# A two-branch attention kernel: where its units of maxima are done, who splits one weight, and which PSUM set serves the query tiles

## Chip, cores and metric

The kernel runs on one core of a Trainium2 chip. The metric is the device time of one execution in microseconds (us); the time before is the median of three runs. Engines: PE multiplies matrices, ACT (ScalarE) does activations and copies, DVE (VectorE) elementwise work and reductions, POOL (GpSimd) elementwise work on SBUF alone, SP (SyncE) issues the DMAs.

## What is computed

`x` has 2048 tokens of 448 numbers, everything in float32. Two attention branches with 16 heads of 28 are mixed by a gate:

```python
g = sigmoid((x * gate_w).sum(-1, keepdims=True))
# branch A: linear attention with learned features
phi_q = concat(softmax(q @ w_phi), softmax(-(q @ w_phi)))      # the same for k
kv = einsum("bhsf,bhsd->bhfd", phi_k, v);  z = phi_k.sum(s)
a = (phi_q @ kv / (phi_q @ z + 1e-6)) @ wo_A
# branch B: full softmax attention, q, k, v from another weight
b = softmax(q @ k.T * 28**-0.5) @ v @ wo_B
return g * a + (1 - g) * b
```

## The kernel before

Tokens are tiled by 128 (16 tiles) or 512 (4 blocks), heads in 4 groups of 4. Precise products are made of two halves: a weight or an input is split into a rounded copy (`high`, on ACT as a rule) and the rest (`low`, a subtraction on DVE as a rule), `split_weight` L140, and three products of the halves are added; a tile of 448 columns is so 11 matmuls (`x3`, `tok_major`).

The order of PE, DVE, ACT and POOL is written out by hand: each engine runs its instructions in the order in which the code emits them. Only SP's queue of DMAs is ordered by a planner. `lows`, `exps`, `subs`, `diffs` are lists of instructions that are emitted later, when `take_lows` and its like are called.

The stages, in order of time:

1. Projections of branch B's q and k (`proj_qk`, n = 4 to 19, L663 on). At n = 16 and 18, `split_part` (L611) splits the two halves of wvA.
2. One loop over i (L726), with t = i the key tiles of branch A (i = 0 to 15) and q = i - 16 the query tiles (from i = 16 on), y = q - 1. A key tile does pk (keys), pva (values and gate), features and their sums into `pkv`. In the first twelve key tiles every second also does one more `proj_qk`.
3. At q = 2, the turn: `kv_copy` takes `pkv`, the pool of PSUM tiles is closed and opened again (L748 to L750) with four banks for the tag "s" in place of three for "s" and one for "pv". The query tiles do pq, features (`features1`: maxima on DVE, subtractions on POOL and, up to q = 8, on DVE; an exponential on ACT; `features2`: sums on DVE, a product on POOL), transposes (`turn`, pft), numerators (`numer`, pn). The numerators are normalized in four steps over the following tiles (`normalize1` to `normalize4`: copies oUa on ACT, denominators dena to DRAM and, repeated, back as rsa, a multiplication oUa on DVE, casts oTa on ACT and subtractions oTa on POOL), and `out_a` (poa, L556) applies the output weight. From q = 18 on, `value_b` (pvb) makes branch B's values of tiles 0 to 7. wvB is split at q = 14 and 17 (L804); its subtractions are emitted one tile later.
4. Last values: `value_b` of tiles 8 to 15 (L909), and the stacks for the scores (memsets, loads).
5. Scores, exponentials and values of branch B over 256 steps (L1115 on); `bank` hands out PSUM banks in the order of the lists `free`, `used`, `held`.

Softmax in branch B needs a maximum for each query ahead of the scores. For the first 44 pieces that is done by `mx_unit` (L258), which is called from stages 1 to 4: four matmuls of 28 rows side by side, two into `pmb`, two into `pmd` (L284), a relu of pmd on ACT (L287), two sums with a running maximum on DVE (L289). pmb and pmd take two PSUM banks each of four, so a unit needs the banks of the unit before. The rest of the maxima is done beside the scores (`mx_visit`, L304). Which unit comes next is counted in `mxs["u"]`; the loads of later pieces (`pair_query`, `mx_query`, `mx_load`) hang on that count. Units 0 to 3 are called at n = 16 to 19, then two for a pair of key tiles (one ahead of the pair, one by `tick` L718 in the middle of its 44 passes), one each at q = 0 and 1, one each at q = 8 to 18, two each from q = 19 on until all are done at q = 24. What is left would be done among the last values (L907 on); there, `psn[1]` is 3, and pmd has a tag of its own.

Of the kernel before, what the change touches and what calls it, by code (L numbers as in the profile page):

```python
# [14 lines left out]
PSUM = bass.MemoryType.PSUM  # L15
# [24 lines left out]
def gated_mix_kernel(ctx, tc, xT, wqkB, wvB, wvA, wkAT, wqAT, phi, woA, woB,  # L40
# [17 lines left out]

    psn = [3, 2]

    def ps_s(nm):
        return ps.tile([P, 512], F32, tag="s", name=nm, bufs=psn[0])

    def ps_pv(nm):
        return ps.tile([P, 512], F32, tag="pv", name=nm, bufs=1)
# [74 lines left out]
    def split_weight(w, raw, bs, cs, low=nc.vector, high=nc.scalar.copy):  # L140

        high(w[:, 0, bs, cs], raw)
        lows.append(lambda: low.tensor_sub(w[:, 1, bs, cs], raw, f32(w[:, 0, bs, cs])))
# [464 lines left out]
    def part_loads(key, src, n, nm):  # L608
        loads(key, lambda: load_part(src, n, nm, 0), lambda: load_part(src, n, nm, 2))

    def split_part(w, key, n, i, low=nc.vector):  # L611
        split_weight(w, raws[key][i], slice(2 * i, 2 * i + 2), slice(0, n), low)

    def splits(n):

# [47 lines left out]
    for n in range(4, NP):  # L663
        take_acts()
        if n in (4, 5):
            x_loads(n - 2)
        if n == 8:
            nc.sync.dma_start(phi_s, phi)
            load_fold(wkAT, "k")
        if n == 10:  # L670
            part_loads("wB1", wqkB[:, :, 512:896], 384, "wB1")
        splits(n + 1)
        if n == 14:
            part_loads("wvA", wvA, 450, "wvA")
            nc.sync.dma_start(sel_s, sel)
            nc.sync.dma_start(mask_s, mask)
            for v in vap:
                nc.gpsimd.memset(v[:, :, 28:32], 0.0)
                nc.gpsimd.memset(v[:, :, 28:29], 1.0)
            feats = [bd.tile([P, H, 64], F32, name=f"feat{i}") for i in range(4)]  # L680
            for f in feats:
                nc.gpsimd.memset(f[:, :, 56:], 0.0)
        if 16 <= n < 20:
            mx_unit()
        proj_qk(n, ev)
        if n in (16, 18):
            split_part(wvA_s, "wvA", 450, (n - 16) // 2)
            take_lows()
        if 12 <= n < 16:
            fold(wkA_s, "k", n - 12)  # L690
        if n == 10:
            pair_query(0, 0)
            pair_load(0, 0)
        if n == 15:
            pair_load(0, 1)
            pair_query(0, 1)
        if n in (14, 19):
            take_subs()
# [27 lines left out]
    for i in range(2 * NT + 11):  # L726
        t, q = i, i - NT
        y = q - 1
        tb = y // 2
        take_acts()  # L730
        if t < NT and t % 2 == 0:
            mx_unit()
            passes = (55 if t < NT - 4 else 44) + (4 if t >= 4 else 0)
            pace["n"], pace["at"] = 4 if t >= 4 else 0, [passes // 2]
        if q in (0, 1):
            take_exps()

        if t % 2 == 0 and 0 <= t - 4 < NT:
            kv_add(t - 4)
            kv_add(t - 3)  # L740
        if q == 2:
            bk_s.close()
            ta_s = ExitStack()
            ta = ta_s.enter_context(tc.tile_pool(name="ta", bufs=1, reuse_waits="tile"))
            stg = ta_s.enter_context(tc.tile_pool(name="stg", bufs=2, reuse_waits="tile"))
            KV = ta.tile([P, 512], F32, name="KV")
            kvT = kv_copy()
            ps_s_.close()  # L748
            ps = ps_s_.enter_context(tc.tile_pool(name="psq", bufs=1, space=PSUM, reuse_waits="tile"))
            psn[0] = 4  # L750
            woA_s = weights(3, "woA_s")
            wvB_s = weights(2, "wvB_s")
            take_exps()
        if t < NT:
            pk = ps_s(f"pk{t}")
            tok_major(pk, t, wkA_s, D, tick)
            fk[t] = features1(pk, f"k{t}", nc.gpsimd)
            take_exps(1)
        if 0 <= q < NT:
            pq = ps_s(f"pq{q}")  # L760
            tok_major(pq, q, wqA_s, D)
        if q == 0:
            fk[NT - 1] = features2(fk[NT - 1], f"k{NT - 1}")
        if q in (1, 2):
            fq[q - 1] = features2(fq[q - 1], f"q{q - 1}")
        if 0 <= q < NT:
            fq[q] = features1(pq, f"q{q}", nc.vector if 0 < q < 9 else nc.gpsimd)
        if 0 <= t - 1 < NT - 1:
            fk[t - 1] = features2(fk[t - 1], f"k{t - 1}")
        if q in (0, 1) or q >= 8:  # L770
            mx_unit()
        if y >= 9 and y % 2 and tb - 4 < 8:
            oTs[tb - 4] = normalize4(ta, num.pop(tb - 4), f"a{tb - 4}", 2)
        if y >= 4 and y % 2 == 0 and tb - 2 < 8:
            numer(tb - 2)
        if q > 0:
            take_exps(int(q < NT))
        if q == 3:
            kv_out(kvT)
        if 2 <= q - 1 < NT:  # L780
            fq[q - 1] = features2(fq[q - 1], f"q{q - 1}")
        take_subs()
        if t == 1:
            pair_load(0, 3)
        if y >= 8 and y % 2 == 0 and tb - 4 < 8:
            num[tb - 4] = normalize3(*num[tb - 4], 2)
        if t < NT:
            value_a(t)
            if t % 2 and t < NT - 4:
                proj_qk(NP + t // 2, ev)  # L790
        if q in (0, 1):
            proj_qk(NP + 6 + q, ev)
        take_lows()
        if 2 <= i < 6:
            fold(wqA_s, "q", i - 2)
        if q == 1:
            ev_s.close()
        if q == 2:
            raws["woA"] = [load_woA(b) for b in (0, 2)]
        if q == 11:  # L800
            part_loads("wvB", wvB, D, "wvB")
        if q in (4, 6):
            split_part(woA_s, "woA", D, (q - 4) // 2)
        if q in (14, 17):  # L804
            split_part(wvB_s, "wvB", D, (q - 14) // 3)
        if q == 1:
            gates()
        if y < 9 or y % 2:
            if y >= 2 and y - 2 < NT:
                turn(y - 2)  # L810
        if 0 <= y - 10 < NT:
            out_a(y - 10)
            out_a2(y - 10)
        if y >= 9 and y % 2 == 0 and y - 2 < NT:
            turn(y - 2)
        if NT + 3 <= q < NT + 10:
            mx_unit()
        if q == NT + 2:
            bd_s.close()
            vb = [value_tile(0)]  # L820
        if 0 <= q - NT - 2 < 8:
            value_b(q - NT - 2)
        if y >= 5 and y % 2 and tb - 2 < 8:
            num[tb - 2] = normalize2(ta, *num[tb - 2], f"a{tb - 2}", 2, True)
# [78 lines left out]
    ps_s_.close()  # L903
    ps = ps_s_.enter_context(tc.tile_pool(name="psv", bufs=1, space=PSUM, reuse_waits="tile"))
    psn[:] = 2, 3
    rlp = fr_s.enter_context(tc.tile_pool(name="rlp", bufs=1, reuse_waits="tile"))
    mx_unit()  # L907
    rest = NF - mxs["u"]
# [17 lines left out]

    free, used, held = list(range(7)), [], []
    spare = []  # L930

    def bank(i, nm):
# [289 lines left out]
```

## Time and profile before

| what | us |
|---|---|
| median of 3 runs (1024.96 to 1025.58) | 1025.13 |
| the profiled execution | 1025.96 |
| its span, from the first to the last instruction | 1024.2 |
| PE busy / DVE / ACT / POOL | 1013.9 / 680.7 / 820.0 / 236.2 |

The times of a timeline count from the span's start; a timeline's row has start, length, engine, line, operation, out<-in, shape and count, and in brackets how long the engine stood idle before it and what ended that. A row of busy time by stages has the stretch, its length, the busy time (and count) of PE, PEld (weight loads), DVE, ACT and POOL, then the mean granted clock of PE, the DMA share and GB/s. Key tiles run from 64 to 171 us, query tiles from 171 on, the last values from 318 to 337, the scores from there to the end.

### The profile page before, as it was taken

Reading aid. Unit: us, or ns where it says so; the run is one execution under the profiler, and the core shown is the slowest. Engines: PE = TensorE matmul, PEld = TensorE weight load, DVE = VectorE, ACT = ScalarE, POOL = GpSimd, SP = SyncE. Lnnn points to the kernel's source line nnn. Section 1 sums busy time; section 2 is a strip of 40 time slices with the busy share of each in tenths; the row PEclk is TensorE's granted clock in tenths of the full one; section 3 lists DMA queues with packets and bytes.
Section 4 is the critical chain, followed back from the end, with each engine's and each line's share of the span. In section 5 each row is a group of like instructions: output and inputs, shape, how many; then the busy total and the mean of one; then the engine's idle time right before and its main releaser. Section 6 shows DMA issues by size and latency. Waiting matters only on the chain.

```text
span 1024.2 us, 18042 instructions
## 1 busy us (share of the span) xinstructions
PE 1013.9 (99%) x6472; PEld 557.3 (54%) x6472; DVE 680.7 (66%) x1340; ACT 820.0 (80%) x1534; POOL 236.2 (23%) x213
## 2 busy tenths in 40 slices
PE   9999999999999999999999999999999999999998
PEld 8878888868779433333333333333333333354555
DVE  6566567987753588788888787887878887710102
ACT  5445445677752999999999999999999999969672
POOL 1245546678435003111011110101201101011010
PEclk9999999989999999999999999999999999999999
DMA  8973110132345713233532133522313355414401
GB/s 297 310 238 93 52 52 1 61 73 81 94 129 132 146 26 77 69 68 72 123 79 72 42 74 74 128 58 55 89 42 77 87 129 140 121 58 125 132 32 54
DMA packets 64250, 98.89 MB, mean 97 GB/s; under 512 B 18176, under 2 KB 24944, under 8 KB 64160
## 3 DMA queue, kind: packets, MB, share of 16 engines
q1 hardware_dynamic: 64160, 97.74, 35.4%
q8 instruction: 51, 0.84, 0.4%
q14 instruction: 39, 0.32, 0.1%
HBM read 69.54 MB, written 27.78 MB: 95 GB/s over the span
## 4 chain that ended last, share of the span: by engine, by line
PE 89%; DVE 4%; DMA 4%; ACT 1%; SPq 1%; issue 1%; POOL 0%; DVEq 0%; ACTq 0%; POOLq 0%
PE st L871 29%; PE pv L998 25%; PE pm L321 9%; PE pk L126 4%; PE pva L126 4%; PE poa L108 4%; PE pob L108 3%; PE pq L108 2%; PE pqk L108 2%; DMA qkd<-ev 2%; PE pvb L126 2%; PE pvb L108 2%; PE pmb L284 1%; PE pft L524 1%; DVE rl L289 1%; DMA wvA_raw<-in_wvA_dram 1%
## 5 line engine op out<-in xcount | busy, mean ns | idle before, releaser
L889 ACT ACTIVATE p<-st 128x512 f32<-128x512 f32 x1020 | 525.7, 609 | 29.5 <-PE st L871 27.9
L332 DVE TENSOR_REDUCE part<-pm 128x1 f32<-128x512 f32 x477 | 304.8, 686 | 111.1 <-PE pm L321 104.7
L871 PE MATMUL st<-qst,kst 128*128 128x512 f32 x1024 | 315.5, 430 | 0.5 <-ACT vb L714 0.5
L998 PE MATMUL pv<-p,vb 128*32 128x512 f32 x2048 | 272.7, 605 | 0.0
L871 PEld LDWEIGHTS st<-qst,kst 128*128 128x128 f32 x1024 | 173.0, 187 | 137.5 <-issue 75.8
L321 PEld LDWEIGHTS pm<-kc,qc 28*128 28x128 f32 x848 | 40.5, 181 | 177.8 <-ACT p L889 169.4
L325 ACT ACTIVATE rl<-pm 128x512 f32<-128x512 f32 x212 | 126.9, 599 | 11.0 <-PE pm L321 0.3
L419 POOL TENSOR_TENSOR oUb<-oUb,rsb 128x512 f32<-128x512 f32 x15 | 19.3, 1289 | 467.4 <-DMA rsb<-rdb 229.9
L329 DVE CUSTOM_DVE_ANT_0 rl<-pm,rl 128x512 f32<-128x512 f32 x159 | 108.3, 681 | 0.0
L321 PE MATMUL pm<-kc,qc 28*128 28x512 f32 x848 | 107.1, 495 | 0.0
L998 PEld LDWEIGHTS pv<-p,vb 128*32 128x32 f32 x2048 | 40.3, 108 | 67.3 <-issue 63.1
L289 DVE CUSTOM_DVE_ANT_0 rl<-pmb,rl 128x512 f32<-128x512 f32 x88 | 57.1, 686 | 29.4 <-ACT rl L287 29.4
L1009 DVE SCALAR_TENSOR_TENSOR acc<-pob,gate,acc 128x448 f32<-128x448 f32 x12 | 8.2, 684 | 86.2 <-PE pob L108 86.2
L108 PE MATMUL pqk<-XH,wB 128*128 128x512 f32 x192 | 59.3, 397 | 0.0
L287 ACT ACTIVATE rl<-pmd 128x1024 f32<-128x1024 f32 x44 | 45.2, 1028 | 12.2 <-PE pmd L284 5.6
L588 ACT CAST ev<-pqk 128x512 fp32r<-128x512 f32 x28 | 16.1, 588 | 36.1 <-PE pqk L108 30.2
L108 PE MATMUL poa<-woA_s,oTa 128*128 128x448 f32 x192 | 43.2, 374 | 0.0
L108 PEld LDWEIGHTS pqk<-XH,wB 128*128 128x128 f32 x192 | 35.4, 188 | 8.5 <-issue 1.5
L108 PE MATMUL pq<-wqA_s,XH 128*128 128x448 f32 x128 | 38.1, 381 | 0.8 <-DVE ev L589 0.8
L195 POOL TENSOR_TENSOR kc<-kc,kd 28x512 fp32r<-28x512 f32 x12 | 15.4, 1281 | 101.9 <-PE pm L321 50.7
L108 PEld LDWEIGHTS poa<-woA_s,oTa 128*128 128x128 f32 x192 | 35.1, 188 | 6.0 <-issue 3.3
L589 DVE TENSOR_TENSOR ev<-pqk,ev 128x512 fp32r<-128x512 f32 x28 | 19.0, 690 | 28.4 <-ACT ev L588 28.3
(159 smaller groups left out, 1176.8 us busy)
## 6 DMA issues: line engine op xcount, KB each, us to landing
qkd<-ev SPq DMA_DIRECT2D x28, 512.0 KB
qst<-qkd SPq DMA_DIRECT2D x64, 224.0 KB
kst<-qkd SPq DMA_DIRECT2D x64, 224.0 KB
od<-oTb SPq DMA_DIRECT2D x48, 112.0 KB
rsa<-rda SPq DMA_DIRECT2D x8, 512.0 KB
rsb<-rdb SPq DMA_DIRECT2D x15, 256.0 KB
kc<-qkd SPq DMA_DIRECT2D x64, 56.0 KB
gad<-ga SPq DMA_DIRECT2D x16, 224.0 KB
```

The lines of the kernel that those rows point to most:

```text
L108: nc.tensor.matmul(dst, l, r, start=i == 0, stop=i == len(todo) - 1)
L126: nc.tensor.matmul(dst[:, :n], l, r, start=i == 0, stop=i == len(todo) - 1, skip_group_check=True)
L287: nc.scalar.activation(rl, pd, AF.Relu)
L289: nc.vector.tensor_tensor_reduce(rl[:, i, :], pb[:, i, :], rl[:, i, :], 1.0, LOWEST, ALU.add, ALU.max, part[:, col + i:col + i + 1])
L321: nc.tensor.matmul(pm[j], mxs[("qc", gq)][js, qt * P:(qt + 1) * P], mxs[("kc", g, kb)][js, :], start=True, stop=True, tile_position=(32 * ...
L325: nc.scalar.activation(rl, pm[kb], AF.Relu if kb < 3 else AF.Copy)
L329: nc.vector.tensor_tensor_reduce(r, pm[j], r, 1.0, LOWEST, ALU.add, ALU.max, part[:, col + j:col + j + 1])
L332: nc.vector.tensor_reduce(part[:, col + j:col + j + 1], pm[j], AX.X, ALU.max)
L419: (nc.gpsimd if n == 1 else nc.vector).tensor_mul(oU, oU, rs)
L871: nc.tensor.matmul(st, kst_of[(g, kt // 4)][:, j, (kt % 4) * P:(kt % 4 + 1) * P], qst_of[gq][:, j, :], start=True, stop=True)
L889: nc.scalar.activation(p, st, AF.Exp, scale=SCALE)
L998: nc.tensor.matmul(pv[32 * j:32 * j + 32, :], vb[kt // 8][:, kt % 8, 4 * g + j, :], pt[j], start=kt == 0, stop=kt == NT - 1, tile_position ...
```

## The change

- The units: pairs of key tiles 4, 6 and 8 have two units by `tick`, at a third and two thirds of their passes, in place of one in the middle; query tiles 8, 9 and 10 have none; from q = 19 on there is one a tile in place of two. So 41 units are done when the loop ends, and three are left to the last values.
- wvA is split by POOL, both halves.
- wvB is split at q = 13 and 15 in place of 14 and 17.
- At the turn the PSUM pool is kept: every fourth tile that asks for "s" gets the bank of "pv". This ends at the last values.
- `free`, the list from which the first banks of the scores are taken, begins in another order.

```diff
+    turn4 = []
+
     def ps_s(nm):
+        if turn4:
+            turn4.append(nm)
+            if len(turn4) % 4 == 0:
+                return ps_pv(nm)
         return ps.tile([P, 512], F32, tag="s", name=nm, bufs=psn[0])
...
-    def split_part(w, key, n, i, low=nc.vector):
-        split_weight(w, raws[key][i], slice(2 * i, 2 * i + 2), slice(0, n), low)
+    def split_part(w, key, n, i, low=nc.vector, high=nc.scalar.copy):
+        split_weight(w, raws[key][i], slice(2 * i, 2 * i + 2), slice(0, n), low, high)
...
         if n in (16, 18):
-            split_part(wvA_s, "wvA", 450, (n - 16) // 2)
+            split_part(wvA_s, "wvA", 450, (n - 16) // 2, nc.gpsimd, nc.gpsimd.tensor_copy)
             take_lows()
...
             mx_unit()
             passes = (55 if t < NT - 4 else 44) + (4 if t >= 4 else 0)
-            pace["n"], pace["at"] = 4 if t >= 4 else 0, [passes // 2]
+            pace["n"] = 4 if t >= 4 else 0
+            pace["at"] = [passes // 3, 2 * passes // 3] if t in (4, 6, 8) else [passes // 2]
...
-            ps_s_.close()
-            ps = ps_s_.enter_context(tc.tile_pool(name="psq", bufs=1, space=PSUM, reuse_waits="tile"))
-            psn[0] = 4
+            turn4.append("")
...
-        if q in (0, 1) or q >= 8:
+        if q in (0, 1) or q >= 11:
             mx_unit()
...
-        if q in (14, 17):
-            split_part(wvB_s, "wvB", D, (q - 14) // 3)
+        if q in (13, 15):
+            split_part(wvB_s, "wvB", D, (q - 13) // 2)
...
-        if NT + 3 <= q < NT + 10:
-            mx_unit()
...
     psn[:] = 2, 3
+    turn4.clear()
...
-    free, used, held = list(range(7)), [], []
+    free, used, held = [0, 2, 3, 4, 5, 1, 6], [], []
```

## The prediction, made before the run

> **What bounds the kernel now.** I read the page first (busy shares, chain), then busy time by stages, the waits of PE, and the timelines of the other engines where a wait stands. Times are us from the span's start.
>
> ```profile
> PE 1013.9 (99%) x6472; PEld 557.3 (54%) x6472; DVE 680.7 (66%) x1340; ACT 820.0 (80%) x1534; POOL 236.2 (23%) x213
> ...
> PE 89%; DVE 4%; DMA 4%; ACT 1%; SPq 1%; issue 1%; POOL 0%; DVEq 0%; ACTq 0%; POOLq 0%
> ```
>
> ```profile
> 64.00:171.00 107.00, 107.00 (x960) 90.07 (x958) 66.25 (x139) 52.30 (x89) 58.51 (x50) 1.00 0.23 69
> ...
> 211.00:229.00 18.00, 15.90 (x129) 11.61 (x128) 15.32 (x33) 11.91 (x20) 14.45 (x12) 0.81 0.38 97
> ...
> 337.40:1018.00 680.60, 680.48 (x4096) 284.52 (x4097) 462.31 (x928) 631.24 (x1235) 65.30 (x62) 1.00 0.33 82
> ```
>
> PE is busy nearly throughout and is nearly the whole chain. The second view (busy PE, PEld, DVE, ACT, POOL, then the granted clock) shows where it isn't: 211 to 229 has 2.1 us idle and a clock of 0.81. From 337.4 on (scores and values, two thirds of the time) the change touches nothing but the start. PE's work stays the same, so the forecast is a sum over PE's waits before 337.4: which go, which come.
>
> Nearly all are one wait. A unit of maxima is matmuls into pmb and pmd (0.43 of PE in all), a relu on ACT (1.03) and two sums on DVE (1.23). Unhindered, pmd starts beside pmb; hindered, it waits until DVE has left the unit before. A bracket in a row is PE's idle time; it leaves out the 0.5 in which pmb alone ran, so the wait is the bracket + 0.5.
>
> **Part by part.**
>
> *wvA split by POOL.* Units stand 3.2 apart here, and two are held up:
>
> ```profile
> 56.36 0.50 PE L284 MATMUL pmd<-kp,qp 28*128 28x512 f32 x2 [0.68 <-DVE part L289]
> ...
> 63.59 0.50 PE L284 MATMUL pmd<-kp,qp 28*128 28x512 f32 x2 [0.34 <-DVE part L289]
> ```
>
> ```profile
> 53.01 0.95 ACT L142 CAST wvA_s<-wvA_raw 128x900 fp32r<-128x900 f32 x1 [0.34 <-DMA wvA_raw<-in_wvA_dram]
> ```
>
> ```profile
> 58.41 2.66 POOL L220 TENSOR_TENSOR kp<-kp,kt 28x512 fp32r<-28x512 f32 x2 [10.87 <-DMA kt<-qkd]
> ```
>
> ```profile
> L428 POOL TENSOR_TENSOR oTb<-oUb,oTb 128x512 fp32r<-128x512 f32 x15 | 19.3, 1287 | 1.2
> ...
> L427 POOL CAST oTb<-oUb 128x512 fp32r<-128x512 f32 x15 | 9.2, 613 | 0.9
> ```
>
> The waits are 1.18 + 0.84 = 2.0. Without ACT's cast and DVE's subtraction between its steps, a unit is through in 3.0, and they go. POOL, idle for 10.9 before 58.41, takes the work: scaled by columns (900/512) a cast is about 1.0 and a subtraction 2.3, so two of each from 53.0 end at 59.5, and the subtractions of kp queued behind them at 62.1. The first key tile's unit needs those and would start at 61.6: a new wait of 0.5. Net **-1.5**; bounds -2.0 (no wait) and 0 (POOL a third slower).
>
> *Three more units on key tiles 4 to 9*: **+1.3** of PE (3 x 0.43). Their cover:
>
> ```profile
> 113.16 0.50 PE L284 MATMUL pmb<-kp,qp 28*128 28x512 f32 x2
> ...
> 120.23 0.50 PE L284 MATMUL pmb<-kp,qp 28*128 28x512 f32 x2
> ```
>
> ```profile
> 115.44 0.69 DVE L289 CUSTOM_DVE_ANT_0 rl<-pmb,rl 128x512 f32<-128x512 f32 x1
> ```
>
> A unit is through 3.0 after its start (113.16 to 116.1), and they stand 7.1 apart. With three a pair they stand 4.5 to 5.1 apart, and two of the three now come right behind a key tile's copy, exponentials, maxima and sums, which I add up to 3.8 and 4.3. That fits, by 0.2 at the tightest; I take no wait.
>
> *The turn and query tiles 8 to 10.* Rows of PE, DVE, ACT, POOL and of the DMAs:
>
> ```profile
> 183.91 0.68 PE L108 MATMUL pq<-wqA_s,XH 128*128 128x448 f32 x2 [0.83 <-DVE ev L589]
> ...
> 206.95 0.50 PE L284 MATMUL pmb<-kp,qp 28*128 28x512 f32 x2
> ...
> 210.64 0.50 PE L284 MATMUL pmb<-kp,qp 28*128 28x512 f32 x2
> 213.25 0.79 PE L284 MATMUL pmd<-kp,qp 28*128 28x512 f32 x2 [2.10 <-DVE part L289]
> ...
> 221.38 1.10 PE L524 MATMUL pft<-ident,feat 128*128 128x128 f32 x8
> ...
> 225.11 1.11 PE L538 MATMUL pn<-fT,KV 56*32 56x256 f32 x32
> 226.15 2.73 PE L108 MATMUL poa<-woA_s,oTa 128*128 128x448 f32 x12
> 228.71 1.04 PE L524 MATMUL pft<-ident,feat 128*128 128x128 f32 x8
> ```
>
> ```profile
> 211.89 0.68 DVE L289 CUSTOM_DVE_ANT_0 rl<-pmb,rl 128x512 f32<-128x512 f32 x1
> ...
> 213.12 1.07 DVE L458 TENSOR_REDUCE fsumq<-feat 128x32 f32<-128x896 f32 x1
> ...
> 217.92 1.09 DVE L458 TENSOR_REDUCE fsumq<-feat 128x32 f32<-128x896 f32 x1 [0.71 <-ACT feat L451]
> ...
> 219.31 1.16 DVE L419 TENSOR_TENSOR oUa<-oUa,rsa 128x1024 f32<-128x1024 f32 x1
> ...
> 257.61 2.59 DVE L143 TENSOR_TENSOR wvB_s<-wvB_raw,wvB_s 128x896 fp32r<-128x896 f32 x1
> ```
>
> ```profile
> 208.36 0.53 SPq L413 DMA_DIRECT2D rsa<-rda  x1
> ```
>
> ```profile
> 268.16 0.54 SPq L413 DMA_DIRECT2D rsa<-rda  x1
> ```
>
> ```profile
> 276.69 1.22 DVE L419 TENSOR_TENSOR oUa<-oUa,rsa 128x1024 f32<-128x1024 f32 x1 [1.07 <-DMA rsa<-rda]
> ```
>
> ```profile
> 222.55 1.13 ACT L427 CAST oTa<-oUa 128x512 fp32r<-128x512 f32 x2
> ...
> 224.43 1.06 ACT L527 COPY fT<-pft 128x512 f32<-128x512 f32 x2
> ```
>
> ```profile
> 224.12 2.53 POOL L428 TENSOR_TENSOR oTa<-oUa,oTa 128x512 fp32r<-128x512 f32 x2
> ```
>
> ```profile
> 213.00:219.70 6.70, 6.45 (x48) 4.57 (x49) 5.89 (x15) 3.91 (x6) 3.66 (x4) 0.50 0.39 104
> ```
>
> Keeping the PSUM set takes away the 0.83 at 183.91, for DVE too. The units of tiles 8 and 9 take with them the 2.6 wait at 213.25 and what followed: the clock at 0.50 for the next 6.7. These add up to 6.7 (0.83, 2.6 and half of 6.5). Then what is late next? DVE is. It lags already: the unit started at 206.95 has its sums at 211.89. Its multiplication at 219.31 moves up by 0.83, two units (2 x 1.23) and the idle 0.71, to 215.3. But it needs rsa, which took 8.5 from issue (268.16 to 276.69): 208.36 - 0.83 + 8.5 = 216.0. Behind it, in ACT's order, stand the casts, an exponential and the copies of fT (222.55 to 225.49, so 2.9), and behind those pn. So pn starts at 216.2 + 1.2 + 2.9 = 220.3. PE is there at 218.1: 210.64 less 0.83 and one unit is 209.4; 4.3 for pn, transposes and a query tile; 3.7 (221.38 to 225.11); 0.7 of small waits for features. The gap is **2.2**, as long as the one that went. POOL then has features and two subtractions (2.53) until 223.3, and poa ends at 224.6 instead of 228.71. If POOL's next product gets in ahead of DVE's multiplication (the 2.59 row shows such a delay: the larger multiplication above it took 1.16), it is 222.1 and 225.8. So this stage gives 4.1 or 2.9, mean 3.5, at full clock. As a gap of 2.1 halved the clock, I let 2.2 do so: 6.8 at half clock cost 3.4, of which 0.7 was waiting anyway. Left: **-0.8**, between -4.1 and +0.2.
>
> *wvB split earlier; fewer units in the output tiles.*
>
> ```profile
> 261.48 0.50 PE L284 MATMUL pmd<-kp,qp 28*128 28x512 f32 x2 [0.58 <-DVE part L289]
> ...
> 279.65 0.49 PE L284 MATMUL pmb<-kp,qp 28*128 28x512 f32 x2
> 280.25 0.50 PE L284 MATMUL pmd<-kp,qp 28*128 28x512 f32 x2
> ...
> 304.97 0.49 PE L284 MATMUL pmb<-kp,qp 28*128 28x512 f32 x2
> 305.13 0.50 PE L284 MATMUL pmd<-kp,qp 28*128 28x512 f32 x2
> ```
>
> The 1.08 at 261.48 came from the split at 257.61; moved to tiles without a multiplication it finds DVE free: **-1.1**. The second unit of a tile waits from 0.60 (first) to 0.16 (last), six times, 1.6 in all; one unit a tile, 5 apart, doesn't: **-1.6**. Three units fewer there: **-1.3**. At nothing: SP's queue, whose moved loads of qp, kc and qc all stand ahead of their use by over 10 us.
>
> *Last values*:
>
> ```profile
> 337.36 2.27 ACT L889 ACTIVATE p<-st 128x512 f32<-128x512 f32 x4
> ```
>
> Three units (1.3). The first comes 2.9 behind the last tile's (0.15 of wait); their sums stand behind DVE's memsets, but the first scores' bank is free 1 us early; the last relu goes ahead of the copies on ACT that the scores' exponentials follow (0.3). **+1.7**. The new order of first banks only renames: banks are laid out in the order of first use. 0.
>
> Sum: -1.5 + 1.3 - 0.8 - 1.1 - 1.6 - 1.3 + 1.7 = **-3.3**. The span of 1024.2 becomes 1020.9 (its run took 1025.96, the median is 1025.13); the median becomes **1021.8**.
>
> **The rivals.** *The clock stays full* behind the gap at pn: the stage gives 3.5, the sum is -6.0, **1019.1**. For it: the 0.83 gap halved nothing, and one of 2.2 may fall differently into what the chip counts. Against it: 2.1 did halve it. [...]
>
> *The gains are passed on*: POOL's split at its bound (0) and the stage at its bound (+0.2) leave -0.8: **1024.3**. For it: ACT, DVE and POOL are 65 to 85% busy from 211 to 229 and hand each wait on.
>
> *Slower: the key tiles hold up their third unit.* If a unit there is through only after 6.2, as the one from 206.95 to 213.1, then two of three wait 1.7 or more, six times: +10, **1032**. It decides from 5.1 a unit on (3.3 over six waits, above 4.5). Against it: from 64 to 171 DVE is busy for 66 of 107, and three units more make it 70.
>
> *It does nothing*: true of the banks alone.
>
> **How the numbers follow.** Forecast 0.57, full clock 0.20, gains passed on 0.14, key tiles 0.09. A measurement can tell 0.2%, 2.05 us, from no change: 1023.1. Of the forecast's cases 0.05 lie above that, beside the 0.13 of the third and 0.01 above. Faster 0.72, same 0.18, slower 0.10. The range goes from the full clock with DVE's multiplication ahead of POOL's product (4.1 in place of 3.5), 1018.5, to the passed-on case, 1024.3.
>
> **What would show it.** Right: no pmd wait near 56, 64, 184, 213, 261 and 280; a PE gap of about 2 at the first pn behind the first multiplication by rsa, with casts on ACT as the releaser's neighbours, and a clock of 0.5 after it; key tiles without waits. Wrong: waits of pmd in the key tiles; POOL's subtractions of kp later than 63; a full clock (then 1019); a start of the scores less than 1 us earlier.

## The result, and the profile after

| what | before | after |
|---|---|---|
| median, us (8 runs each) | 1025.3 (1024.84 to 1026.83) | 1021.91 (1021.34 to 1023.28) |
| ratio, 95% interval | | 0.9967 [0.9956, 0.9978] |
| the profiled execution / its span | 1025.96 / 1024.2 | 1022.5 / 1020.7 |

The kernel became 3.4 us faster (interval 2.3 to 4.5), which is what the prediction gave (-3.3, 1021.8). The profile of after shows that the sum came out of terms several of which were wrong.

The page of after: busy times and the chain by engine. Little has changed (PE is 93% of the chain where it was 89%).

```profile
PE 1011.9 (99%) x6472; PEld 555.4 (54%) x6472; DVE 679.0 (67%) x1338; ACT 817.3 (80%) x1532; POOL 241.9 (24%) x217
...
PE 93%; DVE 3%; DMA 2%; ACT 0%; POOL 0%; issue 0%; DVEq 0%; SPq 0%; POOLq 0%; ACTq 0%
```

Busy time by stages of after (stretch, length, busy time and count of PE, PEld, DVE, ACT, POOL, granted clock, DMA share, GB/s): the key tiles are still free of idle time, and 211 to 229 has 2.7 us idle where before had 2.1, at a clock of 0.91 where it was 0.81.

```profile
64.00:171.00 107.00, 107.00 (x904) 88.77 (x902) 68.16 (x149) 53.54 (x90) 57.42 (x49) 1.00 0.23 69
211.00:229.00 18.00, 15.28 (x132) 11.67 (x117) 15.65 (x26) 11.06 (x20) 14.44 (x13) 0.91 0.33 86
```

To see which stage gave what, I cut both spans at the same matmuls. PE's timeline of before at the cuts (183.91 and 228.71 stand in the prediction):

```profile
48.79 0.50 PE L284 MATMUL pmb<-kp,qp 28*128 28x512 f32 x2
...
64.01 0.47 PE L126 MATMUL pk<-wkA_s,XH 128*128 128x448 f32 x1
...
171.01 0.47 PE L108 MATMUL pq<-wqA_s,XH 128*128 128x448 f32 x1
...
270.29 0.57 PE L108 MATMUL pvb<-wvB_s,XH 128*128 128x448 f32 x2
...
317.55 0.57 PE L126 MATMUL pvb<-wvB_s,XH 128*128 128x448 f32 x2
...
338.42 0.64 PE L998 MATMUL pv<-p,vb 128*32 128x512 f32 x4
```

and of after, with the unit ahead of the key tiles and the turn between them:

```profile
49.76 0.50 PE L290 MATMUL pmb<-kp,qp 28*128 28x512 f32 x2
...
62.77 0.50 PE L290 MATMUL pmd<-kp,qp 28*128 28x512 f32 x2
63.20 0.47 PE L132 MATMUL pk<-wkA_s,XH 128*128 128x448 f32 x1
...
172.15 0.67 PE L114 MATMUL pq<-wqA_s,XH 128*128 128x448 f32 x2
...
184.15 0.68 PE L114 MATMUL pq<-wqA_s,XH 128*128 128x448 f32 x2
...
227.08 0.49 PE L530 MATMUL pft<-ident,feat 128*128 128x128 f32 x3
...
269.24 0.57 PE L114 MATMUL pvb<-wvB_s,XH 128*128 128x448 f32 x2
...
313.60 0.67 PE L132 MATMUL pvb<-wvB_s,XH 128*128 128x448 f32 x2
...
334.76 0.64 PE L1002 MATMUL pv<-p,vb 128*32 128x512 f32 x4
```

The differences of these starts, here and for the kernels of the experiments (cut in the same way; us):

```
              first unit  key     query tiles to   to first     output  last
              to pk       tiles   first poa's end  value tile   tiles   values
before        15.22       107.00  57.70            41.58        47.26   20.87
after         13.44       108.95  54.93            42.16        44.36   21.16
b_units       15.50       108.92  57.52            41.63        48.57   21.31
b_rest        14.04       106.92  54.89            44.28        46.53   20.86
b_turn        14.78       106.98  54.66            41.58        47.73   20.87
b_norm        13.43       107.02  54.89            41.59        46.50   20.86
d_wvB         13.50       106.98  54.89            41.23        47.90   20.86
a_wvB_late    13.44       108.95  54.93            41.84        45.33   21.30
a_den5        13.46       108.91  54.97            42.97        45.48   21.45
a_norm        13.44       108.91  54.97            41.38        44.36   21.15
a_banks       14.38       108.89  54.95            42.31        44.38   21.31
a_fill        14.67       108.91  54.92            42.29        45.39   21.45
a_woA         13.43       108.91  55.73            42.19        45.21   21.30
c_best        14.03       108.84  55.71            41.21        44.35   21.16
```

After against before: -1.78, +1.95, -2.77, +0.58, -2.90, +0.29, and from the first values to the end of the span +0.20. ("First poa's end" is cut at the start of the transposes behind it.) The first unit came 0.97 later; that is a difference of the executions (in the 14 profiles it starts between 48.5 and 50.0, whatever the kernel). The six stages add up to -4.6; with the late start and the end that is -3.5, the difference of the spans.

What PE waited for in after, from 171 us on (total, times, longest):

```profile
PE pft L530 <- POOL feat L466: 2.3, 1, 2.3
PE pmd L290 <- ACT fT L533: 0.7, 1, 0.7
PE poa L114 <- POOL oTa L434: 0.3, 1, 0.3
```

The waits of pmd in the output tiles and of pq at the turn are gone, as foreseen. But the gap of 2.3 stands at transposes, not at pn, and there is a wait of pmd (0.7) that the prediction had taken away. (Its row names a copy on ACT; the loads of the same matmuls' weights name DVE's sums, L295, and the text below goes by these.) The row at 62.77 shows a rest of 0.2 in the first stage.

**What a unit costs in a row of full passes.** PE's timeline of after around the first of the new units:

```profile
94.33 0.36 PE L132 MATMUL pva<-wvA_s,XL 128*128 128x450 f32 x1
94.53 0.36 PE L132 MATMUL pva<-wvA_s,XH 128*128 128x450 f32 x1
94.83 0.50 PE L290 MATMUL pmb<-kp,qp 28*128 28x512 f32 x2
...
95.26 0.47 PE L132 MATMUL pva<-wvA_s,XH 128*128 128x450 f32 x1
95.57 0.36 PE L132 MATMUL pva<-wvA_s,XL 128*128 128x450 f32 x1
```

From start to start a pass takes 0.20 (94.33 to 94.53). Ahead of the unit it is 0.30, the unit itself 0.43, and the pass behind it 0.31. So a unit costs 0.64: its own 0.43 and 0.1 at each seam. Three of them are the +1.95 of the key tiles, in which nothing waited.

**Where the query stage was held.** The timeline of after, all engines, from tile 8's features to the first poa:

```profile
209.45 1.71 POOL L466 TENSOR_TENSOR feat<-feat,fsumq 128x896 f32<-128x896 f32 x1 [0.73 <-DVE fsumq L465]
209.48 2.62 DVE L149 TENSOR_TENSOR woA_s<-woA_raw,woA_s 128x896 fp32r<-128x896 f32 x1 [0.18 <-issue]
...
217.41 1.09 PE L530 MATMUL pft<-ident,feat 128*128 128x128 f32 x8 [2.32 <-POOL feat L466]
...
218.71 1.53 DVE L425 TENSOR_TENSOR oUa<-oUa,rsa 128x1024 f32<-128x1024 f32 x1 [0.40 <-DMA rsa<-rda]
219.12 2.69 POOL L466 TENSOR_TENSOR feat<-feat,fsumq 128x896 f32<-128x896 f32 x1
220.28 1.14 ACT L433 CAST oTa<-oUa 128x512 fp32r<-128x512 f32 x2 [3.70 <-DVE oUa L425]
...
223.57 2.52 POOL L434 TENSOR_TENSOR oTa<-oUa,oTa 128x512 fp32r<-128x512 f32 x2
...
224.89 1.29 PE L114 MATMUL poa<-woA_s,oTa 128*128 128x448 f32 x5 [0.34 <-POOL oTa L434]
```

DVE's second subtraction for woA started 0.03 behind POOL's product and took 2.62. The first, of the same shape, took 1.09 (201.07), and there POOL's product, 0.22 behind it, was the long one (2.43, where the row above has 1.71). The second was through 0.94 behind the product's end (209.45 + 1.71 = 211.16), so I take the 1.5 that it was longer for waiting. The features are late by that, and POOL then works without a break from 215.66 to its subtractions for oTa, which the first poa waits for.

**Where the gain of wvB went.** The timeline of after, all engines, around query tile 17:

```profile
254.98 0.55 SPq L419 DMA_DIRECT2D rsa<-rda  x1
255.62 1.14 SPq L407 DMA_DIRECT2D dena<-oUa  x2
...
260.50 1.54 DVE L149 TENSOR_TENSOR wvB_s<-wvB_raw,wvB_s 128x896 fp32r<-128x896 f32 x1
...
263.64 0.18 DVE L413 TENSOR_SCALAR dena<-dena 128x32 f32<-128x32 f32 x1 [1.60 <-DMA dena<-oUa]
...
264.12 0.63 DVE L295 CUSTOM_DVE_ANT_0 rl<-pmb,rl 128x512 f32<-128x512 f32 x1
```

The last row is the first sum of the unit that started at 258.80. It could have begun at 262.04; it stands behind dena in DVE's order, and dena's 8 KB come 8 us after their issue (255.62 to 263.64), behind rsa's 512 KB in SP's queue. The next unit waits 1.2 for these sums.

### The profile page after: what moved, and what is told of

It is laid out like the page before. It is cut to its first block, busy times and chain, and to the rows that moved or that the text cites. A ratio compares the mean times of both kernels' runs of the same rounds, so it can differ in the third digit from the quotient of the medians.

```text
span 1020.7 us, 18046 instructions
## 1 busy us (share of the span) xinstructions
PE 1011.9 (99%) x6472; PEld 555.4 (54%) x6472; DVE 679.0 (67%) x1338; ACT 817.3 (80%) x1532; POOL 241.9 (24%) x217
## 4 chain that ended last, share of the span: by engine, by line
PE 93%; DVE 3%; DMA 2%; ACT 0%; POOL 0%; issue 0%; DVEq 0%; SPq 0%; POOLq 0%; ACTq 0%
PE st L874 29%; PE pv L1002 25%; PE pm L327 9%; PE pqk L114 6%; PE pk L132 4%; PE pva L132 4%; PE pob L114 3%; PE poa L114 3%; PE pvb L132 2%; PE pvb L114 2%; PE pmb L290 2%; PE pq L114 1%; PE pqk L657 1%; DMA dena<-oUa 1%; PE pkv L484 1%; DMA gad<-ga 1%
## 5 line engine op out<-in xcount | busy, mean ns | idle before, releaser
L295 DVE CUSTOM_DVE_ANT_0 rl<-pmb,rl 128x512 f32<-128x512 f32 x88 | 56.6, 681 | 35.3 <-ACT rl L293 35.3
L1002 PEld LDWEIGHTS pv<-p,vb 128*32 128x32 f32 x2048 | 40.3, 108 | 67.2 <-issue 62.6
L114 PE MATMUL poa<-woA_s,oTa 128*128 128x448 f32 x192 | 43.7, 375 | 0.3 <-POOL oTa L434 0.3
```

Of the source, the lines that this page charges most:

```text
L114: nc.tensor.matmul(dst, l, r, start=i == 0, stop=i == len(todo) - 1)
L295: nc.vector.tensor_tensor_reduce(rl[:, i, :], pb[:, i, :], rl[:, i, :], 1.0, LOWEST, ALU.add, ALU.max, part[:, col + i:col + i + 1])
L1002: nc.tensor.matmul(pv[32 * j:32 * j + 32, :], vb[kt // 8][:, kt % 8, 4 * g + j, :], pt[j], start=kt == 0, stop=kt == NT - 1, tile_position ...
```

## The experiments

The times are ratios to runs of the kernel before made beside them, in four groups of runs (b_units, b_rest, a_wvB_late and a_den5 in one; a_norm, a_banks, a_fill and a_woA; b_turn, b_norm and c_best; d_wvB alone); a_ kernels are edits of after, b_, c_ and d_ as said. The stages of an experiment come from one profiled execution. The stages are in the table above.

**The moves of units alone** (b_units), on the kernel before:

```diff
-            pace["n"], pace["at"] = 4 if t >= 4 else 0, [passes // 2]
+            pace["n"] = 4 if t >= 4 else 0
+            pace["at"] = [passes // 3, 2 * passes // 3] if t in (4, 6, 8) else [passes // 2]
...
-        if q in (0, 1) or q >= 8:
+        if q in (0, 1) or q >= 11:
...
-        if NT + 3 <= q < NT + 10:
-            mx_unit()
```

> The kernel before with only the moves of units (key tiles 4 to 9 get three more, query tiles 8 to 10 and the second place in the output tiles get none). Theory: the parts add. Read off the two profiles, a unit between full passes costs 0.64 us (0.44 of its own and 0.1 at each seam), so key tiles +1.9; the query stage -1.9 (the wait of 2.6 behind the unit of tile 9 goes, the 0.83 at the turn stays, and the load of rsa still sets the first poa); output tiles -3.3; last values +0.9: together -2.4 us, ratio 0.9976. Rival, the terms of the prediction: key tiles +1.3 and last values +1.7 for 0.43 a unit, and the first split of wvA keeps its two waits: -1.6 to -4 with the query stage anywhere between. The stages of the profile tell them apart: the distance from the unit before to the unit behind each third unit grows by 0.6 or by 0.43.

0.9996 [0.9984, 1.0009]: no gain that can be told from none. The key tiles cost 1.92, so a unit costs 0.64. The rest of the theory fell: the parts don't add. The query stage gave 0.2 instead of 1.9, because the gap came back as 3.3 us at pn with the clock at half for 6.8 us behind it. In the output tiles the profiled execution (the longest of the ten, 1029.97) lost 1.3 instead of winning 3.3; the timeline of b_units shows by what:

```profile
292.49 0.18 DVE L407 TENSOR_SCALAR dena<-dena 128x32 f32<-128x32 f32 x1 [8.47 <-DMA dena<-oUa]
...
294.28 0.50 PE L284 MATMUL pmd<-kp,qp 28*128 28x512 f32 x2 [2.20 <-DVE part L289]
```

DVE stands 8.5 us at dena with sums behind it, the next unit waits, and the clock falls once more.

**All but the moves of units** (b_rest), on after:

```diff
-            pace["at"] = [passes // 3, 2 * passes // 3] if t in (4, 6, 8) else [passes // 2]
+            pace["at"] = [passes // 2]
...
-        if q in (0, 1) or q >= 11:
+        if q in (0, 1) or q >= 8:
...
+        if NT + 3 <= q < NT + 10:
+            mx_unit()
```

> The kernel before with everything but the moves of units: wvA split by POOL, the PSUM set kept at the turn, wvB split in tiles 13 and 15, the list of first banks. Theory: wvA -1.8; the turn -0.8, since the chain dena, rda, rsa that ends in the first poa starts earlier by the same; wvB 0, since the unit behind the split waits for dena's landing, which stays where it was; banks 0: -2.6 us, ratio 0.9975. Rival 1: the 0.83 at the turn is swallowed by the wait of the unit in tile 9, which then grows from 2.6 to 3.4: -1.8. Rival 2, the prediction's term: wvB gives 1.1: -3.7.

0.9983 [0.9970, 0.9995], that is -1.7 us, with the theory's -2.6 and rival 1's -1.8 both inside the interval. wvA gave 1.2 and the query stage 2.8, though the units of tiles 8 and 9 stayed. With wvB in tiles 13 and 15 the stage behind the first poa became 2.7 longer: a unit waited 1.8 behind dena, and the clock was at half for 3.4 us after it. So wvB's term isn't -1.1, nor the 0 of the theory, and the turn's 0.8, in theory and rival 1, was too small for the stage.

**wvB late again** (a_wvB_late):

```diff
-        if q in (13, 15):
-            split_part(wvB_s, "wvB", D, (q - 13) // 2)
+        if q in (14, 17):
+            split_part(wvB_s, "wvB", D, (q - 14) // 3)
```

> The kernel after with wvB split in tiles 14 and 17 again. Theory: what holds the unit of query tile 18 is dena, which lands 8 us after its issue because it stands behind rsa's 128 packets of 4 KB in the same queue; VectorE waits for it whatever stands before it. So the wait of 1.2 moves from that unit back to the one of tile 17 and the place of the first unit in the output tiles stays within 0.3 us: time +-0.3 us. Rival (the prediction's term): the place of the split is worth 1.1 us, and the time grows by 1.1.

0.9972 [0.9963, 0.9981], beside 0.9967 and (a_banks) 0.9979 for after: no difference, though the interval is too wide to exclude the rival's 1.1. The stages decide: the wait moved back to the unit of tile 17, and the stage is 0.3 shorter where the rival has it 1.1 longer. The theory's forecast held for this stage, but not its reason: in the late place it is wvB's subtraction itself (255.66, 2.59 long) that stands ahead of the sums, not dena. The output tiles are 1.0 longer: a unit at 287.8 waits 0.98 behind dena, for which DVE stands idle for 6.9. In after DVE stands 5.7 at the same place, and no unit is held.

**dena by another queue** (a_den5):

```diff
-            nc.sync.dma_start(den[:, i, :], oU[DH:P:32, i, :])
+            (nc.scalar if nm == "a5" else nc.sync).dma_start(den[:, i, :], oU[DH:P:32, i, :])
```

> The kernel after with one pair of small DMAs (dena of the sixth pair of query tiles) issued by ScalarE behind its copies, instead of from SyncE's queue behind rsa. Theory: dena lands some 4 us earlier, VectorE's idle 1.6 us ahead of its sums goes, the unit of query tile 18 doesn't wait its 1.2 us, and all that follows comes 1.2 us earlier: -1.2 us, ratio 0.9988 against the kernel after. Rival: what holds that unit is VectorE's subtraction for wvB and its contention with GpSimd; then the idle time goes but the sums come only 0.3 us earlier, and the time stays.

0.9976 [0.9967, 0.9986]: no gain. DVE's idle 1.6 went, but ACT's order paid for it. The timeline of ACT in a_den5:

```profile
251.93 2.00 ACTq L407 DMA_DIRECT2D dena<-oUa  x2
```

Two DMA issues held ACT for 2.0 us, the features (253.98) and copies behind them came late, and the stage is 0.8 longer than in after. The expectation missed this: it had left out what the issue itself costs on the engine that issues. And the sums still come 5.0 behind their unit's start (5.3 in after), as the rival had it, for DVE's step on dena, 0.18 long in after, now takes 1.68 and ends with POOL's product. The timelines of a_den5, POOL and DVE:

```profile
261.71 2.43 POOL L466 TENSOR_TENSOR feat<-feat,fsumq 128x896 f32<-128x896 f32 x1
```

```profile
262.50 1.68 DVE L413 TENSOR_SCALAR dena<-dena 128x32 f32<-128x32 f32 x1
```

They end at 264.2 and 264.1. In after the same product ends at 263.61 (261.05 + 2.56), just as dena's landing lets the step begin, so I estimate that with dena there in time the step would hardly have been through earlier.

**The sums ahead of dena** (a_norm). This takes away the same wait by order alone:

```diff
         if q in (0, 1) or q >= 11:
             mx_unit()
+        while behind:
+            behind.pop(0)()
...
-            num[tb - 2] = normalize2(ta, *num[tb - 2], f"a{tb - 2}", 2, True)
+            def den(b=tb - 2):
+                num[b] = normalize2(ta, *num[b], f"a{b}", 2, True)
+            if y >= 15:
+                behind.append(den)
+            else:
+                den()
```

> The kernel after with VectorE's two steps on dena (add and reciprocal, and the DMAs behind them) emitted behind the next unit instead of ahead of it, from query tile 16 on. Theory: in the last query tiles and the output tiles a unit waits because VectorE, ahead of the sums of the unit before, stands waiting for dena, which lands 8 to 10 us after its issue. With the sums first, VectorE's idle 1.6 us at dena comes after them, the unit of query tile 18 loses its wait of 1.2 us, and no unit of the output tiles has sums later than 3 us after its start (3.8 in one tile of the kernel after): -1.2 us, ratio 0.9988 against the kernel after. Rival: rda and rsa start later by the same, the multiplication by rsa and with it the output tiles become late: poa waits, and the time is the same or up to 2 us longer.

0.9959 [0.9946, 0.9971]; 1021.23 (five runs) beside 1022.87 of a_banks (eleven) in the same group, so 1.6 us shorter where 1.2 were expected; the two intervals just touch. The timeline of a_norm, DVE:

```profile
261.52 0.68 DVE L295 CUSTOM_DVE_ANT_0 rl<-pmb,rl 128x512 f32<-128x512 f32 x1
...
263.42 0.18 DVE L413 TENSOR_SCALAR dena<-dena 128x32 f32<-128x32 f32 x1 [0.60 <-DMA dena<-oUa]
```

The sums come 3.2 behind their unit's start in place of 5.3, no unit waits after 171 us, and the stage is 0.8 shorter. That the step on dena, standing ahead of the sums, held them is shown by this. Whether its DMA or POOL's product held the step isn't told apart: a_den5, with the DMA out of the way, moved the sums by 0.3 alone.

**The list of first banks** (a_banks):

```diff
-    free, used, held = [0, 2, 3, 4, 5, 1, 6], [], []
+    free, used, held = list(range(7)), [], []
```

> The kernel after with the list of first banks in its old order. Theory: banks are laid out in the order of their first use, so the list only renames them: the time of the kernel after, ratio 1.000, and every stage as long as there. Rival: the first scores get banks that come free at another time, and the stage from the last value tile to the first values differs by some 0.5 us.

0.9979 [0.9970, 0.9987], its interval overlapping that of after, and every stage within 0.15 of after's except the first (14.38; see wvA in the next section). The instructions of all five engines are the same in the same order as in after, so this is also a second measurement of after itself, and its profile differs in one thing: the clock. Busy time by stages of after, in two stretches of 3.41 us, the gap in the first:

```profile
215.24:218.65 3.41, 1.24 (x10) 1.23 (x11) 3.01 (x7) 1.33 (x3) 2.99 (x3) 1.00 0.38 101
218.65:222.07 3.42, 3.42 (x11) 2.76 (x9) 2.58 (x3) 1.79 (x3) 3.42 (x3) 0.50 0.11 15
```

and of a_banks, where the same gap of 2.3 us lies across the border of two such stretches:

```profile
213.01:216.42 3.41, 1.79 (x9) 1.31 (x7) 3.34 (x7) 2.35 (x4) 1.40 (x2) 1.00 0.69 181
216.42:219.83 3.41, 2.70 (x17) 2.59 (x18) 3.38 (x6) 0.68 (x2) 3.41 (x3) 1.00 0.16 34
```

In a_banks the clock stayed full, and the query stage took 54.95 where it took 54.93 at half clock. PE then only waits longer for POOL (PE's timeline of a_banks):

```profile
224.64 2.34 PE L114 MATMUL poa<-woA_s,oTa 128*128 128x448 f32 x10 [1.23 <-POOL oTa L434]
```

So in after the half clock costs this stage nothing.

**The gap filled** (a_fill), ahead of the transposes of tile 7:

```diff
+        if q == 10:
+            fill = ps_mx("fill", False)
+            for _ in range(11):
+                nc.tensor.matmul(fill[:, 0, :D], XH[:, 0, :P], XH[:, 0, :D], start=True, stop=True)
```

> The kernel after with eleven more matmuls of 128x448 in the gap of 2.3 us ahead of the transposes that wait for GpSimd; nobody reads their result. Theory: without the gap the clock doesn't fall to 0.5, the query tile behind it takes 2.3 us in place of 4.0; but the first poa waits for GpSimd's subtraction in any case, so its end comes at most 0.4 us earlier: the half clock was hidden. -0.4 us at the most, 0 in the timing. Rival 1: the half clock costs its 1.7 us, and the end of the first poa comes 1.7 us earlier. Rival 2: the clock falls by another count than idle time, and the half clock stays.

0.9986 [0.9977, 0.9995]. In the profile the clock stayed full, and the query stage took 54.92, as expected. That it isn't faster agrees with a_banks. As a whole it is rather slower (1023.65 beside 1022.87 of a_banks): the output tiles are 1.0 longer, by the wait behind dena of a_wvB_late, which a_den5 and a_woA have too (0.8 to 1.1). And in six of its ten runs the mean clock is 0.998, with a median of 1024.19 against 1022.36 in the four above: by that the clock did fall there, at a place where it costs, and no trace shows which.

**The lost race undone** (a_woA): the second cast for woA stays, its subtraction comes three tiles later.

```diff
-        if q in (4, 6):
-            split_part(woA_s, "woA", D, (q - 4) // 2)
+        if q == 4:
+            split_part(woA_s, "woA", D, 0)
+        if q == 6:
+            nc.scalar.copy(woA_s[:, 0, 2:4, :D], raws["woA"][1])
+        if q == 8:
+            lows.append(lambda: nc.vector.tensor_sub(
+                woA_s[:, 1, 2:4, :D], raws["woA"][1], f32(woA_s[:, 0, 2:4, :D])))
```

> The kernel after with VectorE's second subtraction for woA done three query tiles later, behind the first multiplication by rsa, so that it doesn't stand ahead of the features (it took 2.6 us there behind GpSimd's product). Theory: what sets the end of the first poa is rsa's landing (VectorE idle 0.4 us for it at 218.7 us), so the gap leaves the transposes and comes back at the first pn, 2 us long, where the prediction had put it; the end of the first poa moves by less than 0.5 us. Rival: the lost race is the cause, and the end of the first poa comes 1.6 us earlier (the part of the subtraction that was waiting).

0.9984 [0.9975, 0.9993]. The gap did leave the transposes, and stands as 1.6 us at pn, where the prediction had put it. But the clock then was at half for 6.8 us, right where the first poa runs, and the stage ended 0.8 later, not within 0.5, nor 1.6 earlier as the rival had it. So the lost race sets the place of the gap, and that place hides the half clock.

**The PSUM set kept, alone** (b_turn), on the kernel before, with `turn4` in `ps_s` as in the change:

```diff
-            ps_s_.close()
-            ps = ps_s_.enter_context(tc.tile_pool(name="psq", bufs=1, space=PSUM, reuse_waits="tile"))
-            psn[0] = 4
+            turn4.append("")
```

> The kernel before with only the PSUM set kept at the turn. Theory: nearly all of the gain of the query stage is this one part: the seven profiles with the set kept have the first poa end 42.9 us (one 43.7) after the third query tile's start, the two without it 44.7, with or without units in tiles 8 to 10, with or without the half clock. So the turn gives 0.9 at once and 1.9 more up to the first poa's end, and the rest stays: -2.8 us, ratio 0.9973. Rival 1, the prediction's terms: 0.8 at the turn, and the 2.6 of the unit of tile 9 with its half clock stay: -0.8 us, ratio 0.9992. Rival 2: the waits for dena in query tiles 16 to 18 eat what comes earlier: the stage behind the first poa is longer by up to 2.7, as in the kernel with all but the moves of units, ratio 0.999 to 1.000.

0.9987 [0.9977, 0.9997], -1.3 us (0.3 to 2.4): the theory's 2.8 lies outside, rival 1's 0.8 inside. The profile shows the theory's stage (54.66, -3.0) and 0.5 given back in the output tiles; but it was one of two among the twelve runs whose mean clock was 0.999 and not below. In it a pmd wait of 2.0 lay across the border of two stretches (idle 1.02 and 0.97, the clock 1.00 in both). Rival 2 fell too: the stage behind the first poa is as long as before (41.58). What makes the stage long in before seems to be the half clock, as ACT's timelines show, before and then b_turn:

```profile
221.05 0.53 ACT L440 COPY pcq<-pq 128x448 f32<-128x448 f32 x1 [2.19 <-PE pq L108]
221.63 1.03 ACT L287 ACTIVATE rl<-pmd 128x1024 f32<-128x1024 f32 x1
```

```profile
217.92 0.53 ACT L446 COPY pcq<-pq 128x448 f32<-128x448 f32 x1 [0.35 <-PE pq L114]
218.50 1.03 ACT L293 ACTIVATE rl<-pmd 128x1024 f32<-128x1024 f32 x1
219.58 1.14 ACT L433 CAST oTa<-oUa 128x512 fp32r<-128x512 f32 x2
```

Before: ACT waits 2.2 us for a query tile that PE does at half clock, and the relu and the casts (222.55) stand behind it, though DVE's product was there at 220.47. In b_turn nothing of this. Of the 2.8 that separate before from b_rest, the turn is 0.9 (its third query tile starts 12.0 behind the first, in before 12.9).

The runs agree. One stretch of 3.41 us at half clock takes, by my estimate, 0.0017 off the mean clock of a run (1.7 of some 1022), so 0.998 fits one stretch and 0.997 two. Of 89 runs of the kernel before in the four groups, the 8 with 1.000 have a median of 1024.15, the 60 with 0.998 of 1025.59 and the 16 with 0.997 of 1026.64: there the half clock costs some 1.4 or 2.5. The profiled execution of before has two stretches, so its query stage is longer than that of most runs. Of the eleven runs of a_banks, the 4 with 1.000 have 1022.73, the 7 below 1023.06: a cost like that of before isn't seen there. No trace shows before with a full clock, so that the rest of the stage's gain, 1.9, is the clock's is argued from these runs, not shown.

**No unit moved** (b_norm): b_rest with wvB late and with a_norm's edit.

```diff
-        if q in (13, 15):
-            split_part(wvB_s, "wvB", D, (q - 13) // 2)
+        if q in (14, 17):
+            split_part(wvB_s, "wvB", D, (q - 14) // 3)
...
+        while behind:
+            behind.pop(0)()
...
```

> The kernel before with the PSUM set kept, wvA split by GpSimd and VectorE's steps on dena behind the next unit from tile 16 on; no unit is moved and wvB stays in tiles 14 and 17. Theory: turn -2.8, wvA -1.2 to -1.8, and no wait for dena in front of sums: -4.3 us, ratio 0.9958, beside the kernel after with the same reordering (0.9959 in five rounds): then the moves of units bring less than 0.6 us, what is saved in the output tiles being paid in the key tiles and the last values. Rival: the moves of units carry 2 us or more of the gain, and this kernel is at 0.998 or above.

0.9952 [0.9939, 0.9964], -4.9 us: the expectation (-4.3) held. Without any move of units this is at least as fast as after (0.9967, 0.9979) and as a_norm (0.9959). Three of its five runs had the full clock (median 1020.55), two not (1021.90, 1022.25). The moves of units bring what they cost: -2.1 in the output tiles, +1.9 in the key tiles, +0.3 in the last values (a_norm against b_norm, which differ in wvB's place too). Its ratio is the lowest here, but the intervals of c_best and a_norm overlap it, and of before's runs only 8 in 89 had the full clock that three of its five had.

**Three together** (c_best): a_norm's and a_woA's edits, and:

```diff
+        if q == 11:
+            fill = ps_mx("fill", False)
+            for _ in range(8):
+                nc.tensor.matmul(fill[:, 0, :D], XH[:, 0, :P], XH[:, 0, :D], start=True, stop=True)
         if q in (0, 1) or q >= 11:
             mx_unit()
```

> The kernel after with three things: VectorE's steps on dena behind the next unit from tile 16 on; the second subtraction for woA behind the first multiplication by rsa; and eight matmuls whose result nobody reads ahead of the unit of query tile 11, where TensorE would be idle. Theory: with the subtraction moved, GpSimd's last subtraction ends 0.9 us earlier (41.0 after the third query tile's start against 41.9), but the gap then lies at pn and the clock falls to half during the first poa, which took 6.3 us in place of 2.6; with the gap filled it stays full and the first poa ends at 42.1 in place of 42.9. With the reordering's gain: ratio 0.9951 against before. Rival: the eight matmuls delay the unit and pn by as much as the clock gives, and the ratio is that of the reordering alone, 0.9959, or worse.

0.9954 [0.9942, 0.9966]: the time can't tell the two. The stage can: 55.71, no better than a_woA. 1.5 us of the gap stayed between the unit and pn, the clock fell behind it, and the first poa took 4.8 us. So the theory fell: first poa's end came 43.7 behind the third query tile's start, not 42.1, and the eight matmuls didn't keep the clock full. The rival's time fits as well, but not its reason.

**wvB early without the wait** (d_wvB), on b_norm:

```diff
-        if q in (14, 17):
-            split_part(wvB_s, "wvB", D, (q - 14) // 3)
+        if q in (13, 15):
+            split_part(wvB_s, "wvB", D, (q - 13) // 2)
```

> The kernel with the PSUM set kept, wvA split by GpSimd and the steps on dena behind the next unit, no unit moved, and now wvB split in tiles 13 and 15. Theory: with dena out of the way of the sums, the move of wvB does take away the wait of 1.08 us of the unit of tile 17, but ScalarE, which carries the casts of wvB and the copies that the transposes wait for, hands back most of it: the stage from the first poa's end to the first value tile is 41.4 us in the profile with this move and the reordering, 41.6 without the move; so -0.2 us, ratio 0.995. Rival, the prediction's term: the wait was all there was to gain, and the time is 1.1 us shorter: ratio 0.9941.

0.9964 [0.9951, 0.9977] against b_norm's 0.9952 [0.9939, 0.9964]: no gain. The wait of 1.08 is gone and the stage is 0.4 shorter, but the output tiles are 1.4 longer: there DVE waits 2.6 for rsa, which was issued later, with a unit's sums behind it, and the next unit waits 1.5. Theory and rival both missed what comes after.

## Why the prediction was right, step by step

The total was right; of its steps, three were.

- **wvA by POOL** (-1.5): -1.78. Right, bounds too. But the new wait of 0.5 for POOL's kp didn't come: a subtraction took 1.97, not 2.3, and kp was ready at 61.1 (58.47 + 2.65), ahead of its unit. The rest of 0.2 at 62.77 is a wait for DVE's sums of the unit before, which end at 62.6. The timeline of after, DVE:

```profile
61.93 0.69 DVE L295 CUSTOM_DVE_ANT_0 rl<-pmb,rl 128x512 f32<-128x512 f32 x1
```

  The size depends on the execution: in a_banks, a_fill and b_rest the gain was 0.6 to 1.2. There a copy on ACT ahead of the first unit's relu waited 2.4 to 3.5 for a DMA, and the first or the second unit was held. And without the change, before, b_units and b_turn differ among themselves by 0.7 (14.78 to 15.50).
- **Key tiles** (+1.3, no waits): +1.95. The mechanism was right, the price of a unit was mis-sized: 0.43 was PE's time for its four matmuls, 0.64 is what it takes out of a row of full passes.
- **The turn and query tiles** (-0.8): -2.77. This step failed in two places. "DVE is late next" was right, and a gap of 2.2 was foreseen (2.3), but at pn; a race that DVE lost by 0.03 us put it at the transposes. And "6.8 at half clock cost 3.4, of which 0.7 was waiting anyway": it was 3.4 at half clock, all of it beside POOL's work, which sets the end (a_banks, a_fill). The gain at full clock was sized too high as well: rsa landed 10.0 after its issue (208.69 to 218.71), not 8.5, and the prediction goes on from 216.2 where its own sum gives 216.0. At full clock the stage gave 2.75 (a_banks), not the mean of 3.5. So the rival of a full clock was mis-priced too: its -6.0 can't be had, since the full clock comes out at the same end.
- **wvB** (-1.1): +0.58 for the stage. That the split made the 1.08 is right (a_wvB_late, b_norm). "Finds DVE free" failed: in the new place DVE's step on dena stands ahead of the sums (a_norm). With dena out of the way the 1.08 does go (d_wvB), and a wait for rsa takes its place in the output tiles.
- **Output tiles** (-1.6 and -1.3): -2.90, with two units fewer (9 in place of 11). The third, the first of the three that were left, is done at 313.17, just ahead of the cut; counted with the last values it makes this -3.3: units at 0.64 in place of 0.43, and the waits. Right, but near an edge: in a_wvB_late, a_den5, a_fill and a_woA a wait behind dena takes back 0.8 to 1.1.
- **Last values** (+1.7): +0.29, or +0.7 with that unit. Too much. The three units do cost 0.64 each, but a wait of 0.5 at the first scores of before is gone, and the passes of the value tiles took 0.203 each in place of 0.207, 0.35 in all. In a_banks, with the same instructions, the mean is 0.2045, so it isn't the kernel that sets it alone. Why they did stays open.
- **Banks** (0): 0.

The errors were -0.3, +0.6, -2.0, +1.7, 0 to -0.4, -1.0 to -1.4. They come to -1.3 in all: the six stages gave -4.6 where -3.3 was forecast. That the spans differ by no more than 3.5 is owed to the start of after's execution, 1.0 late, and before's profiled execution has more of the half clock than most of its runs. So that the total came out within 0.1 is luck. Of the gain of 3.4, the moves of units carry little by themselves (b_units), and b_norm does without them. What they may do is to take away the exposure of the query stage to the half clock; that is worth some 1.4 to 2.5 in the runs in which the clock falls, and nothing in the others. That this is so in runs without a trace is read from their mean clock, not shown.

## What to carry to other kernels

When a wait of the bottleneck engine is taken away, look at what stands next in the order of the engine that released it: here a step that waits for a DMA, or is held by another engine, stood ahead of sums whose data were there, and putting it behind them gave more than moving the load. A short piece of work put between full passes cost its seams here as well as its own time (0.64 us, not 0.43). What a stall cost in clock went by where it fell: behind the gap of 2.3 us after had 3.41 us at 0.50 and a_banks none, and the query stage, which waits for POOL in any case, took 54.93 and 54.95.

## What the hardware showed

- **The clock changed on a grid of 3.413 us.** The trace's record of the clock begins at full clock, at 4.71 in before and 7.03 in after. The clock fell to half 208.21 and 211.63 behind that, which is 61 and 62 times 3.4133, and stayed there for 6.83 and 3.41, two of them and one. PE's idle time in the stretch just ahead was 1.78 in before (209.51 to 212.92) and 2.17 in after; 1.61 in a_woA (216.50 to 219.91) and 1.30 in b_rest (261.67 to 265.09) were followed by half clock too, 1.62 in a_banks (213.01 to 216.42) and 1.08 in b_rest (207.06 to 210.47) were not. What else counts there stays open.
- **A step of 32 columns on DVE ended with POOL's product.** The timeline of after, POOL and DVE:

```profile
249.40 2.55 POOL L466 TENSOR_TENSOR feat<-feat,fsumq 128x896 f32<-128x896 f32 x1
...
250.31 1.67 DVE L413 TENSOR_SCALAR dena<-dena 128x32 f32<-128x32 f32 x1
```

  It takes 0.18 at 263.64; here it took 1.67 and was through at 251.98, POOL's product at 251.95.
- **A small DMA behind a large one in the same queue was late.** dena's 8 KB, issued behind rsa's 512 KB, landed 8.0 and 8.6 us after issue in after (255.62 to 263.64, 278.08 to 286.66) and 9.6 in b_units (282.90 to 292.49); issued ahead of rsa (at 265.47 in after) it was in use 2.9 later. Issued by ACT it was there in time (DVE idle no more ahead of its step in a_den5), at 2.0 us of ACT for two issues.
